# Spacing the loads of a scan by their landings, and reloading 112 of 128 rows

## The chip, the cores and the metric

One core of one Trainium2 chip. The metric is device time of one execution in microseconds, the median over runs; lower is better. The kernel before took 630.66 us (three runs, 629.27 to 634.14).

## The reference

A recurrent attention with a delta rule is followed by a mixture of experts. For 4 batches and 8 heads, 768 steps and head dimension 40, a 40 x 40 state is carried along the steps:

```
y[t]  = r[t] @ state
Sa    = state @ a[t]
state = state * w[t] - outer(Sa, b[t]) + outer(v[t], k[t])
```

The rows y of all batches and steps form x (3072 x 320). Each row picks one of 8 experts by the largest of `x @ w_gate`, takes a place among that expert's rows in order of arrival, goes through `relu(x @ w1[e]) @ w2[e]` (hidden width 1024), and is scaled by its softmax weight.

## The kernel before

**The scan** works on six stages of 128 steps (index `i`, `NI` = 6), each in two halves of 64 steps (`c`) and for two groups of heads and batches (`pr`). Within a half, matrices of 64 x 64 replace the step by step recurrence. For each (`pr`, `i`) the inputs come as w (tile `px`), a (tile `a`), k and b (tile `kb`, one load for each half) and r (tile `rv`), each a load of 512 KB or a little more, 128 rows of 4 KB. For each (`pr`, `i`, `c`) v comes as two loads of 128 KB (tile `vu`). VectorE makes running products of w (two scans, L494 and L503) and multiplies them into a (L508) and kb (L513); TensorE forms the products (`nn` and `kk`, L406); VectorE inverts a triangular matrix in many small steps (L641, L646); then TensorE carries the states (`zz`, `sa`, `mT`, `yy`). At a stage's end x goes to HBM (`store_x`, two stores of 192 KB each).

Of the 128 rows of w, a and kb the arithmetic on VectorE uses rows 0 to 103 (`R` = 104): two blocks of 40 rows at 0 and 64. In a and kb the rows 104 to 127 are zeros from the host, and products on TensorE read all 64 rows of a block, zeros included. In w the rows between the blocks are copies that keep the values finite.

**The experts** follow: weights are loaded, split in two half-precision parts by ScalarE and VectorE, x is gathered and transposed by DMA, and TensorE multiplies (L1594 and L1463). The first loads of weights go out while the scan still runs.

**The order** of all steps is written out by hand in `ORDER` (L29). `Schedule.listed` (L202) replays it, so each engine gets its instructions in that order and runs them in that order; costs in the steps' texts, such as `L0>2.0`, are not used when an order is given. All plain loads and stores are issued by SyncE through `Schedule.dma` (L169, the calls show as L171). A load's issue waits for its tile to be free, and everything behind it on SyncE waits too. The first steps that load, in order: w, kb, a, kb, w, kb, a, kb, w, a, v, w, v, rv, v, the gate's weights, a, rv; then, from 33.8 us, kb, kb, kb, w, kb, four stores of zeros (`fill`, xd<-tbl), v, w. The number of buffers is 6 for `px`, 4 for `a`, 2 for `kb`, 2 for `rv` and 4 for `vu` (L365).

The lines that the change touches are `Schedule.__init__` and `dma`, `steps` (L173), the loads in `prep` (L460 to L486) and the step of `store_x` (L1041).

Of the kernel before, what the change touches and what calls it, by code (L numbers as in the profile page):

```python
# [19 lines left out]
P = 128  # L20
C = 64
DIGITS = str.maketrans("", "", "0123456789")


OVERLAP = 0.07
AFTER = {"P": 0.3, "A": 0.05, "V": 0.12, "G": 0.06, "W": 0.06}

# [103 lines left out]
class Schedule:  # L131
# [7 lines left out]
    def __init__(self, nc, bufs, mu, tail, bias, alt=(100.0,) * 3, later={}, given=None):  # L139
        self.nc, self.bufs, self.mu, self.o_tail, self.bias, self.alt = nc, bufs, mu, tail, bias, alt  # L140
        self.later, self.given = later, given
        self.begin = {"A": 12.0, "V": 2.0, "G": 8.0}
        self.threads, self.plan, self.queue, self.pick = {}, [0.0], [], {}

    def get(self, name):
        return self.bufs[name].pop(self.pick[name].pop(0) if self.pick.get(name) else 0)
# [20 lines left out]
            self.nc.vector.tensor_mul(out, in_, m)  # L167

    def dma(self, out, in_):  # L169

        (self.nc.scalar if self.queue.pop(0) == "A" else self.nc.sync).dma_start(out, in_)  # L171

    def steps(self, name):  # L173
        def add(fn, text, needs=(), gives=None, take=(), free=()):
            ops = [[[(y[0], [float(z) - OVERLAP * (y[0] == "V") for z in y[1:].split(">")]) for y in x.split("&")]
                    for x in z.split()] for z in text.split("|")]
            self.threads.setdefault(name, []).append((fn, ops, needs, gives, tuple(take), tuple(free), self.plan[0]))
        return add

# [167 lines left out]
def scan_part(tc, keep, one, psum, w, a, kb, rv, vt, w_gate, wge, xd, lg, ident, up, SX, route, fill):  # L347
    nc = tc.nc
    V, A, G, TT = nc.vector, nc.scalar, nc.gpsimd, nc.tensor
    NI = w.shape[1]  # L350
# [39 lines left out]
             "w": -20.1216, "w_": 0.8755, "x": -104.8416, "x_": -62.5388, "zz": 0.4931}  # L390
    sch = Schedule(nc, free_, MU, O_TAIL, O_BIAS, (1.42109, 1.49794, -0.061783), LATER, ORDER)
    get, put, steps, PLAN, queue = sch.get, sch.put, sch.steps, sch.plan, sch.queue
    engine, copy, scale, dma = sch.engine, sch.copy, sch.scale, sch.dma

    def half(x, n=C):
        return slice(C * x, C * x + n)
# [51 lines left out]
    def masked(out, in_):  # L448
# [7 lines left out]
        else:  # L456
            m = mask[:, None, :] if len(sh) == 3 else mask[:, None, None, :]
            V.tensor_mul(out, in_, m.to_broadcast(sh))  # L458

    def prep(pr, i):  # L460
        T = {"pr": pr, "i": i}
        n = (pr, i)

        def loads(kind, src, rows):
            def go():
                T[kind] = get(kind)
                dma(rows(T[kind]), src[pr, i])
            return go

        def load_kb(c):  # L470
            if not c:
                T["kb"] = get("kb")
            dma(T["kb"][:, c].rearrange("p h z t -> p (h z t)"), kb[pr, i, c])

        def load_w():
            T["px"] = get("px")
            dma(T["px"].rearrange("p h t -> p (h t)"), w[pr, i])

        steps("load_w")(load_w, "L0>2.0", take=["px"], gives=("load_w", n))
        steps("load_a")(loads("a", a, lambda x: x.rearrange("p h t -> p (h t)")), "L0>1.9", take=["a"],  # L480
                        gives=("load_a", n))
        for c in range(2):
            steps("load_kb")(lambda c=c: load_kb(c), "L0>1.9", take=["kb"] * (1 - c), gives=("load_kb", n, c))
        PLAN[0] += HC / 2
        steps("load_rv")(loads("rv", rv, lambda x: x.rearrange("p z u t -> p (z u t)")), "L0>1.9",
                         take=["rv"], gives=("load_rv", n))  # L486
        PLAN[0] -= HC / 2

        def scan_g():
            T["gx"] = get("gx")  # L490
            if i:
                T["g0"] = get("g0")
            V.memset(z2[0:R, :, 0:1], 1.0)
            V.tensor_tensor_scan(T["gx"][0:R, 0:H * (P + 1)][:, ::-1],  # L494
                                 T["px"][0:R].rearrange("p h t -> p (h t)")[:, ::-1],
                                 z2[0:R].rearrange("p h t -> p (h t)")[:, ::-1], 1.0, ALU.mult, ALU.add)

        def scan_p():
            g3 = T["gx"][0:R, 0:H * (P + 1)].rearrange("p (h t) -> p h t", t=P + 1)
            if i:  # L500
                V.tensor_copy(T["g0"][0:R, :], g3[:, :, 1])
            V.reciprocal(z2[0:R, :, 0], g3[:, :, 1])
            V.tensor_tensor_scan(T["px"][0:R].rearrange("p h t -> p (h t)"),  # L503
                                 T["px"][0:R].rearrange("p h t -> p (h t)"),
                                 z2[0:R].rearrange("p h t -> p (h t)"), 1.0, ALU.mult, ALU.add)

        def mul_a():
            engine().tensor_mul(T["a"][0:R], T["a"][0:R], T["px"][0:R, :, 0:P])  # L508

        def mul_kb(c):  # L510
            g = T["gx"][0:R, 1:].rearrange("p (h t) -> p h t", t=P + 1)[:, :, 1:]
            x = T["kb"][0:R, c]
            engine().tensor_mul(x, x, g[:, :, None, half(c)].to_broadcast([R, H, 2, C]))  # L513
            if c:
                put("gx", T["gx"])

        add = steps(f"decay{pr}")
        add(scan_g, "V2.4", take=["gx"] + ["g0"] * (i > 0), needs=[("load_w", n)], gives=("gx", n))
        add(scan_p, "V2.6", gives=("px", n))
        add(mul_a, "V1.22|G2.35", needs=[("load_a", n)], gives=("a", n))  # L520
        add = steps(f"decay_k{pr}")
        for c in range(2):
            add(lambda c=c: mul_kb(c), "V1.15|G2.35", needs=[("px" if c else "gx", n), ("load_kb", n, c)], free=["gx"] * c, gives=("kb", n, c))
        return T
# [454 lines left out]
    def gate(T):  # L979
        pr, i = T["pr"], T["i"]  # L980
        n = (pr, i)
        Q = {}

        def turn_y():
            p = Q["pt"] = get("pp")
            for h in range(H):
                TT.transpose(p[:, h // 4, h % 4 * P:h % 4 * P + R], T["px"][0:R, h, 0:P], ident[0:R, 0:R])  # L987

        def logits():
            p = Q["pl"] = get("p1")  # L990
            for h in range(H):
                mm(p[32 * (h % 4):32 * (h % 4) + 16, 0:P], wge[:, h].rearrange("p x e -> p (x e)"), T["px"][:, h, 0:P], h < 4)

        def parts():
            copy(T["px"][:, 0, 0:P], Q["pl"][:, 0:P])

        def fold():
            mm(Q["pl"][:, P:P + 16], T["px"][:, 0, 0:P], pick, True)
            put("px", T["px"])

        def hv(x):
            return Q["pt"].rearrange("p z (k y) -> p (z k) y", y=P)[:, :, C * x:C * x + D]

        def x_hi():
            Q["x16"] = get("x16")
            for x in range(2):
                copy(Q["x16"][:, x, 0, 0:HD].rearrange("p (h d) -> p h d", d=D), hv(x))

        def x_lo():
            for x in range(2):  # L1010
                V.tensor_sub(Q["x16"][:, x, 1, 0:HD].rearrange("p (h d) -> p h d", d=D), hv(x),
                             Q["x16"][:, x, 0, 0:HD].rearrange("p (h d) -> p h d", d=D))
            put("pp", Q["pt"])

        def x_rest():
            y = Q["x16"]
            copy(y[:, :, 1, HD:], y[:, :, 0, 2 * P:HD])
            copy(y[:, :, 0, HD:], y[:, :, 1, 2 * P:HD])

        def take_logits():  # L1020
            scale(lg[:, i * B + pr:i * B + B:2, :], Q["pl"][:, P:P + 16].rearrange("p (x e) -> p x e", x=2), 1.0 / SX)
            put("p1", Q["pl"])

        def store_x():
            for x in range(2):
                t = (pr + 2 * x) * NI + i
                dma(xd[i == NI - 1][t * P:(t + 1) * P, :], Q["x16"][:, x].rearrange("p a c -> p (a c)"))
            put("x16", Q["x16"])

        add = steps(f"gat{late(i)}{pr}")  # L1030
        done = [("y", (pr, 2 * i)), ("y", (pr, 2 * i + 1))]
        add(turn_y, "P1.0", needs=done, take=["pp"], gives=("turn_y", n))
        more = steps(f"logi{late(i)}{pr}")
        more(logits, "P.5", needs=done + [("wge", 0)], take=["p1"])
        more(parts, "A.25|V.25", needs=[("turn_y", n)])
        more(fold, "P.25", free=["px"])
        more(take_logits, "A.2|V.2", free=["p1"], gives=("logits", n))
        add(x_hi, "A.46 A.46|V.49 V.49", take=["x16"])
        add(x_lo, "V.49 V.49", free=["pp"])
        add(x_rest, "A.3 A.3|G.76 G.76")  # L1040
        add(store_x, "L0>.55&L0>.55", needs=[("fill", 0)] * (i == NI - 1), free=["x16"], gives=("store_x", n))  # L1041

    Ts = {}
    for i in range(NI):
# [26 lines left out]
    for m, G_ in enumerate(sets):  # L1071
        PLAN[0] = G_[-1] * GT + 1.5 * GT
        add = steps(f"rout{late(G_[-1])}")
        L_ = {}
        first, count, place, gates, hot_p, hot_j, fold, index = route(m, G_, L_)
        n = len(G_)
        add(first, f"V{1.1 + .2 * n:.2f}", needs=[("logits", (pr, i)) for pr in range(2) for i in G_] + [("gated", m - 1)] * (m > 0),
            gives=("one_hot", m))
        add(lambda f=count, L=L_: (L.update(ps=get("p1")), f()), "P.5", take=["p1"], gives=("counted", m))
        add(lambda f=place, L=L_: (f(), put("p1", L["ps"])), f"V{.6 + .15 * n:.2f}", needs=[("placed", m - 1)] * (m > 0),  # L1080
            free=["p1"], gives=("placed", m))
# [705 lines left out]
```

## Time and profile before

| | before |
|---|---|
| median of three runs | 630.66 us |
| the profiled execution | 628.57 us |
| its span, first to last instruction | 626.8 us |
| TensorE busy (matmul) | 536.7 us, 86% |
| TensorE instructions, matmuls and weight loads | 12512 and 12512 |
| VectorE instructions | 855 |
| VectorE busy | 415.9 us, 66% |
| ScalarE busy | 279.1 us, 45% |
| mean granted TensorE clock | 0.941 |
| DMA, SyncE's queue | 71.91 MB, 39.4% of 16 engines |
| HBM read | 66.39 MB |

The profiled execution took 1.8 us more than its span. Busy shares are means over a scan in which VectorE and TensorE are both above eight tenths busy, and a last third in which TensorE alone is. PE is TensorE's matmuls, PEld its weight loads, DVE is VectorE, ACT ScalarE, POOL GpSimd, SP SyncE; a q behind the name means the engine's sequencer.

### The profile page before, as it was taken

What the parts mean: (1) busy time and instruction counts of PE and PEld (TensorE: products, weight loads), DVE (VectorE), ACT (ScalarE), POOL (GpSimd) and SP (SyncE); (2) the same over time, 40 slices, a digit from 0 to 9 for tenths busy, and PEclk for the clock granted to TensorE, in tenths of its full rate; (3) what the DMA queues carried; (4) which work ended last, traced back from release to release, by engine and by line L of the source; (5) the groups of instructions that cost most, each with busy time, mean ns of one, the idle gap of its engine ahead of it and who ended that gap; (6) DMA issues with size and microseconds to landing.
All of it is one profiled execution on the core that took longest, in us unless ns stands there. A gap on an engine that the chain in (4) does not pass through costs nothing.

```text
span 626.8 us, 27526 instructions
## 1 busy us (share of the span) xinstructions
PE 536.7 (86%) x12512; PEld 394.2 (63%) x12512; DVE 415.9 (66%) x855; ACT 279.1 (45%) x559; POOL 113.4 (18%) x148
## 2 busy tenths in 40 slices
PE   2476988878899898899899898889999969879995
PEld 1365876667677666777688667656766445535653
DVE  7899987887578877488788857956436555142420
ACT  5246534724364455335745345544247334244221
POOL 7110000101010001001010000414152733506102
PEclk9855998999799998799999988989999999989999
DMA  8672152413442524235122426594588868484001
GB/s 345 179 202 72 35 160 91 140 62 101 158 130 87 158 77 138 76 117 157 60 80 73 142 75 198 132 238 125 98 253 227 237 165 210 109 209 117 21 18 37
DMA packets 67219, 83.22 MB, mean 133 GB/s; under 512 B 30590, under 2 KB 54272, under 8 KB 67092
## 3 DMA queue, kind: packets, MB, share of 16 engines
q1 hardware_dynamic: 63764, 71.91, 39.4%
q0 software_dynamic: 3328, 9.44, 5.2%
q8 instruction: 100, 1.64, 1.1%
q14 instruction: 27, 0.22, 0.1%
HBM read 66.39 MB, written 10.09 MB: 122 GB/s over the span
## 4 chain that ended last, share of the span: by engine, by line
PE 54%; issue 23%; DVE 11%; POOL 5%; DMA 3%; ACT 2%; POOLq 0%; SPq 0%; DVEq 0%; ACTq 0%
PE pp L406 27%; PE pp L1594 6%; PE pp L199 5%; PE p L1463 4%; PE pp L851 3%; POOL out_dram L1469 3%; PE p L199 2%; PE pp L562 2%; PE p L406 2%; PE pp L987 1%; POOL a L1440 1%; PE p L889 1%; DVE gx L494 1%; DVE nu L646 1%; DVE tmp L641 1%
## 5 line engine op out<-in xcount | busy, mean ns | idle before, releaser
L406 PE MATMUL pp<-a,kb 64*64 64x64 f32 x1536 | 36.8, 243 | 21.5 <-DVE a L508 7.9
L1469 POOL DMA_INDIRECT out_dram<-tk,ri x25 | 32.2, 1287 | 119.6 <-ACT tk L1629 95.0
L406 PEld LDWEIGHTS pp<-a,kb 64*64 64x64 f32 x1536 | 31.6, 154 | 29.2 <-issue 11.1
L199 PE MATMUL pp<-ident 128*128 128x512 f16 x126 | 43.0, 416 | 4.1 <-ACT pp L424 3.2
L156 POOL COPY x<-x 128x128 f16<-128x128 f16 x12 | 6.5, 540 | 210.6 <-ACT x L156 191.0
L1440 POOL DMA_INDIRECT a<-xd,ri x25 | 29.3, 1171 | 83.7 <-PE pp L987 73.8
L406 PE MATMUL pp<-vu,bk 128*40 128x104 f32 (+1 forms) x768 | 39.7, 257 | 2.4 <-issue 2.1
L406 PEld LDWEIGHTS pp<-vu,bk 128*40 128x40 f32 x768 | 34.2, 120 | 6.6 <-issue 4.5
L458 DVE TENSOR_TENSOR vu<-pp,mask 128x1024 f32<-128x1024 f32 x24 | 29.3, 1221 | 9.8 <-PE pp L406 9.7
L156 ACT COPY vT<-pp 128x1024 f32<-128x1024 f32 x22 | 22.2, 1014 | 30.4 <-PE pp L851 30.3
L570 ACT ACTIVATE bk<-pp,few 128x320 f32<-128x320 f32 x48 | 22.6, 524 | 29.0 <-PE pp L562 19.8
L406 PE MATMUL pp<-rv,vT 64*64 64x64 f32 x1536 | 29.7, 221 | 5.2 <-issue 3.6
L160 ACT ACTIVATE ns<-pp 32x256 f32<-32x256 f32 (+1 forms) x54 | 24.3, 450 | 21.6 <-PE pp L406 20.7
L1594 PE MATMUL pp<-xT,kb 128*128 128x448 f16 (+2 forms) x192 | 32.2, 306 | 0.0
L1594 PE MATMUL pp<-xT,px 128*128 128x448 f16 (+2 forms) x128 | 28.6, 315 | 3.9 <-DMA xT<-a 3.9
L406 PEld LDWEIGHTS pp<-rv,vT 64*64 64x64 f32 x1536 | 25.6, 134 | 8.1 <-issue 3.8
L851 PE MATMUL pp<-ident,vu 128*128 128x128 f32 x192 | 28.2, 294 | 2.2 <-issue 2.1
L1594 PE MATMUL pp<-xT,vu 128*128 128x448 f16 (+1 forms) x128 | 26.2, 370 | 3.8 <-DVE px L1602 3.8
L494 DVE TENSOR_TENSOR_SCAN gx<-px,z 104x1032 f32<-104x1032 f32 x12 | 27.7, 2308 | 2.4 <-DMA px<-in_w_dram 1.9
L513 DVE TENSOR_TENSOR kb<-kb,gx 104x1024 f32<-104x1024 f32 x22 | 27.1, 1252 | 3.1 <-DMA kb<-in_kb_dram 3.1
L641 DVE TENSOR_TENSOR tmp<-xu,nu 128x60 f32<-128x60 f32 (+11 forms) x138 | 28.0, 227 | 1.5
L646 DVE TENSOR_TENSOR nu<-nu,tmp 128x60 f32<-128x60 f32 (+11 forms) x138 | 27.7, 225 | 1.7
(262 smaller groups left out, 1361.5 us busy)
## 6 DMA issues: line engine op xcount, KB each, us to landing
kb<-in_kb_dram SPq DMA_DIRECT2D x24, 512.0 KB, 4.9
vu<-in_moe_w_dram SPq DMA_DIRECT2D x32, 320.0 KB, 3.6
px<-in_w_dram SPq DMA_DIRECT2D x12, 516.0 KB, 5.9
a<-in_a_dram SPq DMA_DIRECT2D x12, 512.0 KB, 4.0
vu<-in_vt_dram SPq DMA_DIRECT2D x48, 128.0 KB, 3.4
rv<-in_rv_dram SPq DMA_DIRECT2D x12, 512.0 KB, 4.7
px<-in_moe_w_dram SPq DMA_DIRECT2D x12, 512.0 KB, 4.7
xd<-x SPq DMA_DIRECT2D x24, 192.0 KB, 2.9
```

What stands on the lines that cost most here:

```text
L156: (e.copy if e is self.nc.scalar else e.tensor_copy)(out, in_)
L199: self.nc.tensor.matmul(x, self.spare[:, 0:P], self.spare[:, None, :].to_broadcast([P, 2, 2 * P]), start=True, stop=True, skip_group_check ...
L406: TT.matmul(out, l, r, start=start, stop=True, skip_group_check=True)
L458: V.tensor_mul(out, in_, m.to_broadcast(sh))
L494: V.tensor_tensor_scan(T["gx"][0:R, 0:H * (P + 1)][:, ::-1], T["px"][0:R].rearrange("p h t -> p (h t)")[:, ::-1], z2[0:R].rearrange("p h t ...
L513: engine().tensor_mul(x, x, g[:, :, None, half(c)].to_broadcast([R, H, 2, C]))
L641: V.tensor_mul(tv(), diag(s_["xu"])[:, :, t0:t1, s:s + 1].to_broadcast([P, nb, n, m]), diag(s_["nu"])[:, :, s:s + 1, 0:m].to_broadcast([P, ...
L646: V.tensor_add(y, y, tv())
L851: TT.transpose(p[:, x, k * P:k * P + P], U["vu"][:, x, k, C:3 * C], ident)
L1440: nc.gpsimd.indirect_dma_start(out=xt(j)[:c].rearrange("p a c -> p (a c)"), out_offset=None, in_=src[:, :], in_offset=bass.IndirectOffsetO ...
L1469: nc.gpsimd.indirect_dma_start(out=out_v[used[0] % (8 * E)][:, :], out_offset=bass.IndirectOffsetOnAxis(ap=ri.bitcast(U32)[:c, j, 1:2], ax ...
L1594: nc.tensor.matmul(s_["h", f + z][:, :n], l, rr, start=m % 7 == 0 and m < 14, stop=m >= 14)
```

## The change

Two things are changed. First, each step of the scan that loads (`load_w`, `load_a`, `load_kb`, `load_rv`, `load_v`, and the load of the gate's weights), and each `store_x`, waits on SyncE until the last DMA of the second last such step has landed. Steps of loads for the experts and the four stores of `fill` neither wait so nor count. Second, a tile of w, a or kb that has been loaded once with all 128 rows is from then on reloaded in its rows 0 to 111. That holds for 6 of 12 loads of w, 8 of 12 of a and 20 of 24 of kb. The order of the steps is the same.

```diff
+LANDED = mybir.DependencyInfo(mybir.DependencyClass.Sync, mybir.DependencyReason.DATA)
...
+        self.spaced, self.loads = False, [[] for _ in range(3)]
...
     def dma(self, out, in_):
-
-        (self.nc.scalar if self.queue.pop(0) == "A" else self.nc.sync).dma_start(out, in_)
+        x = (self.nc.scalar if self.queue.pop(0) == "A" else self.nc.sync).dma_start(out, in_)
+        if self.spaced:
+            for y in self.loads[0][-1:]:
+                self.tc.add_manual_dep(x.ins, y.name, LANDED, reason="loads are spaced")
+            self.loads[-1].append(x.ins)
+
+    def load(self, fn):
+        self.spaced, self.loads = True, self.loads[1:] + [[]]
+        fn()
+        self.spaced = False
 
     def steps(self, name):
...
+            if name.startswith("load_"):
+                fn = lambda fn=fn: self.load(fn)
...
+    whole = set()
+
     def prep(pr, i):
...
+        def part(kind, x, src):
+            y = slice(0, 112 if kind != "rv" and id(T[kind]) in whole else P)
+            dma(x[y], src[y])
+
         def loads(kind, src, rows):
             def go():
                 T[kind] = get(kind)
-                dma(rows(T[kind]), src[pr, i])
+                part(kind, rows(T[kind]), src[pr, i])
+                whole.add(id(T[kind]))
             return go
 
         def load_kb(c):
             if not c:
                 T["kb"] = get("kb")
-            dma(T["kb"][:, c].rearrange("p h z t -> p (h z t)"), kb[pr, i, c])
+            part("kb", T["kb"][:, c].rearrange("p h z t -> p (h z t)"), kb[pr, i, c])
+            if c:
+                whole.add(id(T["kb"]))
 
         def load_w():
             T["px"] = get("px")
-            dma(T["px"].rearrange("p h t -> p (h t)"), w[pr, i])
+            part("px", T["px"].rearrange("p h t -> p (h t)"), w[pr, i])
+            whole.add(id(T["px"]))
...
-        add(store_x, "L0>.55&L0>.55", needs=[("fill", 0)] * (i == NI - 1), free=["x16"], gives=("store_x", n))
+        add(lambda: sch.load(store_x), "L0>.55&L0>.55", needs=[("fill", 0)] * (i == NI - 1), free=["x16"], gives=("store_x", n))
```

## Rows read from the trace of the kernel before

**Rows 1.** Page, part 4: shares of the chain that ended last, by engine.

```profile
PE 54%; issue 23%; DVE 11%; POOL 5%; DMA 3%; ACT 2%; POOLq 0%; SPq 0%; DVEq 0%; ACTq 0%
```

**Rows 2.** Waits of PE, whole run: us in total, times, longest us.

```profile
PE pp L406 <- issue: 29.6, 33, 2.6
```

**Rows 3.** Chain in order of time, pieces without cause: start us, us.

```profile
97.09 1.58 issue
...
161.32 2.37 issue
...
183.78 1.18 issue
...
250.29 2.56 issue
```

**Rows 4.** DMA by queue (packets, MB, share), whole run, then 25 to 400 us.

```profile
q8 instruction: 100, 1.64, 1.1%
...
q8 instruction: 85, 1.39, 1.5%
```

**Rows 5.** DMA by queue, 156.9 to 161.3 us, then 161.3 to 162.4 us.

```profile
q1 hardware_dynamic: 400, 1.46, 88.8%
...
q8 instruction: 1, 0.02, 5.8%
```

**Rows 6.** Timeline of SP, issues: start us, us, what, count.

```profile
39.70 6.71 SPq L171 DMA_DIRECT2D xd<-tbl  x4
...
89.84 3.04 SPq L171 DMA_DIRECT2D kb<-in_kb_dram  x3
...
155.04 0.33 SPq L171 DMA_DIRECT2D rv<-in_rv_dram  x1
155.42 0.83 SPq L171 DMA_DIRECT2D kb<-in_kb_dram  x1
156.33 0.38 SPq L171 DMA_DIRECT2D px<-in_w_dram  x1
156.77 2.57 SPq L171 DMA_DIRECT2D kb<-in_kb_dram  x2
...
177.44 2.07 SPq L171 DMA_DIRECT2D vu<-in_vt_dram  x2
...
246.96 0.88 SPq L171 DMA_DIRECT2D rv<-in_rv_dram  x1
```

**Rows 7.** DMA issues at 155.5, 156.4 and 156.8: KB, us from issue to landing.

```profile
kb<-in_kb_dram SPq DMA_DIRECT2D x1, 512.0 KB, 5.8
...
px<-in_w_dram SPq DMA_DIRECT2D x1, 516.0 KB, 6.2
...
kb<-in_kb_dram SPq DMA_DIRECT2D x1, 512.0 KB, 7.4
```

**Rows 8.** DMA by queue, 186.5 to 191.7 us, all of it; then PE's timeline.

```profile
q8 instruction: 1, 0.02, 1.1%
...
192.80 0.38 PE L406 MATMUL pp<-vu,bk 128*40 128x104 f32 x4 [0.83 <-issue]
```

**Rows 9.** DMA issues at 1.0 and at 33.9 us, as in rows 7.

```profile
px<-in_w_dram SPq DMA_DIRECT2D x1, 516.0 KB, 3.5
...
kb<-in_kb_dram SPq DMA_DIRECT2D x1, 512.0 KB, 3.8
```

**Rows 10.** Timeline of DVE at the start.

```profile
13.19 2.31 DVE L494 TENSOR_TENSOR_SCAN gx<-px,z 104x1032 f32<-104x1032 f32 x1
...
21.53 2.31 DVE L494 TENSOR_TENSOR_SCAN gx<-px,z 104x1032 f32<-104x1032 f32 x1
25.48 1.92 DVE L755 STREAM_TRANSPOSE xu<-ns 128x1024 f32<-128x1024 f32 x1 [1.64 <-ACT ns L160]
```

**Rows 11.** Waits of DVE, 0 to 400 us, for a load, past the first.

```profile
DVE kb L513 <- DMA kb<-in_kb_dram: 3.1, 1, 3.1
```

**Rows 12.** Waits of SP's own queue, whole run.

```profile
SPq L171 <- PE pp L406: 122.6, 24, 25.8
```

More of the change, by code (lines that the diff above doesn't have):

```diff
@@ L392, in scan_part @@
     get, put, steps, PLAN, queue = sch.get, sch.put, sch.steps, sch.plan, sch.queue
+    sch.tc = tc
     engine, copy, scale, dma = sch.engine, sch.copy, sch.scale, sch.dma
@@ L472, in load_kb @@
                 T["kb"] = get("kb")
-            dma(T["kb"][:, c].rearrange("p h z t -> p (h z t)"), kb[pr, i, c])
+            part("kb", T["kb"][:, c].rearrange("p h z t -> p (h z t)"), kb[pr, i, c])
+            if c:
+                whole.add(id(T["kb"]))
         def load_w():
             T["px"] = get("px")
-            dma(T["px"].rearrange("p h t -> p (h t)"), w[pr, i])
-        steps("load_w")(load_w, "L0>2.0", take=["px"], gives=("load_w", n))
-        steps("load_a")(loads("a", a, lambda x: x.rearrange("p h t -> p (h t)")), "L0>1.9", take=["a"],
+            part("px", T["px"].rearrange("p h t -> p (h t)"), w[pr, i])
+            whole.add(id(T["px"]))
+        steps("load_w")(load_w, "L0>1.75", take=["px"], gives=("load_w", n))
+        steps("load_a")(loads("a", a, lambda x: x.rearrange("p h t -> p (h t)")), "L0>1.68", take=["a"],
                         gives=("load_a", n))
         for c in range(2):
-            steps("load_kb")(lambda c=c: load_kb(c), "L0>1.9", take=["kb"] * (1 - c), gives=("load_kb", n, c))
+            steps("load_kb")(lambda c=c: load_kb(c), "L0>1.68", take=["kb"] * (1 - c), gives=("load_kb", n, c))
         PLAN[0] += HC / 2
```

## The prediction

> **What bounds the kernel now.** I read the chain that ended last first: by engine it is TensorE for half, and "issue" for almost a quarter [rows 1], that is time in which an engine waited for nothing that the profile names. The waits of PE tell whose: its matmuls stood 33 times for such a reason, 29.6 us in all [rows 2]. The chain in order of time shows that the long ones in the scan lie on the path [rows 3]. Next I asked what DMA does beside them. Queue 8 moves nothing but instructions, 100 packets of 16 KB, 85 of them between 25 and 400 us, one each 375 / 85 = 4.4 us [rows 4]. Only TensorE has instructions in that number, 25,000 of them. The gap at 161.32 then reads so: from 156.9 to 161.3 us only SyncE's queue moves, 400 packets, and not one of queue 8; the code packet comes just when the gap begins, and PE goes on 1.3 us after that packet's window ends [rows 3, 5]. So TensorE ran out of code, and the code came behind loads. The reader is to see five loads issued between 155.04 and 159.3 [rows 6].
>
> Loads as data are hardly waited for: behind the very first, VectorE waits for one in the whole scan, a kb, for 3.1 us [rows 11]. It is that of 155.42, in the same stretch as PE's gap, and the path there goes over PE [rows 3]. So the change is worth what it does to the code.
>
> **The change part by part.**
>
> (1) Loads kept apart. Before, loads leave as soon as their tiles are free; after, at most two steps are under way. What one transfer holds up is read from the burst: issue plus time to landing gives 155.42 + 5.8 = 161.2, 156.33 + 6.2 = 162.5 and 156.77 + 7.4 = 164.2, so each load of 512 KB takes 1.3 to 1.7 us behind the one before [rows 6, 7]. Three of the long gaps fall where more than two load steps were under way: 97.09 (three kb in a row from 89.84), 161.32, and 183.78 (two v from 177.44 between a w and an rv) [rows 3, 6]. They sum to 1.58 + 2.37 + 1.18 = 5.13 us. The new wait takes one transfer out from before the fetch in the first and third, two at 161.32: at most 1.3 + 2.37 + 1.18 = 4.85 us. The least is nothing: if the fetch was asked for before the later loads were issued, nothing is taken from before it. A fetch with no load beside it still costs something: between 186.5 and 191.7 us queue 8 alone has a packet, and PE stands 0.83 us after it [rows 8]. I take the gaps down to that: 0.75 + 1.54 + 0.35 = 2.6 us, the row nearest to a fetch that finds a short queue. All of it is on the path [rows 3]. The gap of 2.56 us at 250.29 has one rv ahead, from 246.96, and a store of x before it, which the new wait lets pass [rows 3, 6]; it stays, and so do most of the 33.
>
> (2) 112 rows. One eighth less of a load is 1.3 / 8 = 0.16 us. The 34 loads that shrink are a quarter of the 134 DMAs of the steps concerned. If each of the 33 gaps [rows 2] had one of them ahead, the gain would be 5.3 us; if none, zero. A quarter of 33 gives 8 x 0.16 = 1.3 us, which I take. VectorE's, ScalarE's and TensorE's work on the rows is the same and costs the same.
>
> (3) The start. The first nine loads are w, kb, a, kb, w, kb, a, kb, w; each now leaves as the one two before it lands. With t for a load's time to landing, the second w lands at 4.3 + 2t and the third at 4.3 + 4t. VectorE begins on them at 13.19 and 21.53 [rows 10], so nothing is late while t stays under 4.45 and 4.3 us. Loads with few beside them took 3.5 and 3.8 [rows 9]; at 3.8 the two land at 11.9 and 19.5. I take zero. If that cover went, with t = 5.8 as in the burst [rows 7], the second w would be 2.7 late; the third would be 6.0 late, of which 2.7 are in already and 1.64 are VectorE's own idle time before 25.48 [rows 10]: 2.7 + 1.7 = 4.4 us in all.
>
> (4) The second burst, from 33.8 us: kb, w and kb wait for one another, and the four stores of zeros behind them, which SyncE took 6.71 us to issue from 39.70 on, start later [rows 6]. By two loads of 1.3, that is 2.6 us. Nothing reads the zeros soon, and the v and w queued behind them are the next stage's. But a fetch of code then meets these stores where it met none. Between 0 and 2.6 I take 1.0 us against the change, the size of a fetch's lone gap of 0.83 [rows 8] rounded up.
>
> (5) Everything else at nothing. SyncE already stands 122.6 us for TensorE to free tiles [rows 12]; outside the bursts the second last load has landed by then, and the new wait is over before the old one. Behind a waiting load on SyncE stand later loads, stores of x and, late in the scan, loads of weights for the experts, whose tiles come free one by one as well. What VectorE, ScalarE and TensorE are given does not change, and neither does its order.
>
> Sum: -2.6 - 1.3 + 0 + 1.0 = -2.9 us. The profiled execution of 628.57 would become 625.7. It lies 2.1 us under the median of the runs; against the median, 630.66 - 2.9 = 627.8 us.
>
> [...]
>
> **The rivals.**
>
> More than forecast: the depth of the queue is what holds the code up everywhere. Then (1) and (2) give their upper ends, 4.85 + 5.3, and (4) nothing: 630.66 - 10.2 = 620.5 us. For it: PE's gaps are on the path, and 33 of them. Against it: the gaps at 192.80 and 250.29 had no or hardly any load too many [rows 3, 8].
>
> [...]
>
> Slower: apart, loads are slower. Two at a time and 3.8 us for each pair is 1.9 us a load against 1.3 [rows 7, 9]. A burst of five loads then lasts 9.5 us and not 6.5. It decides when a burst outlasts two distances of fetches, 8.8 us [rows 4]: a third fetch then meets traffic, in each of the five stages after the first. At the size of the smallest of the chain's gaps, 1.18 us [rows 3], that is 5.9 us, with no gain elsewhere: 636.6 us. Against it: a fetch has at most two loads ahead, and PE runs some us on the code it has.
>
> **How the numbers follow.** Forecast 0.45, more 0.25, no change 0.18, slower 0.12. The time is the forecast's, 627.8. The range goes from 621, close to the second case, over the third to 634, where the start's 4.4 us or part of the slower case are in; it leaves out some 0.18. About 1%, 6.3 us, is what runs of this kernel can tell from no change. Faster by more than that, under 624.4, is most of the second case and a little of the first: 0.25. Slower, over 637, is half of the last case and a little for a shift of the order that nobody sees in the trace: 0.10. Within: 0.65.
>
> **What would show it.** (1) is right if the gaps without cause near 97, 161 and 184 shrink to under a microsecond and the sum of rows 2 falls by 3 to 5 us; wrong if the code packets come as late as before. (2): kb, w and a of 448 KB land some tenths earlier. (3) is wrong if VectorE's scans near 13 and 21 us wait for a load. (4) shows as a new gap of PE between 45 and 55 us. The prediction falls if the sum of rows 2 halves, or if it grows with more and smaller gaps.

## The result and the profile after

| | before | after |
|---|---|---|
| median, first comparison (20 runs each) | 629.73 us | 629.37 us |
| median, second comparison (29 and 12 runs, the run e1 below) | 631.89 us | 625.39 us |
| the profiled execution | 628.57 us | 630.85 us |
| waits of PE without cause, all tiles | 32.6 us | 32.7 us |
| PE busy, matmul | 536.7 us | 533.1 us |
| HBM read | 66.39 MB | 64.16 MB |

The ratio after to before is 0.9891, 95% interval 0.9849 to 0.9932, in the first comparison and 0.9898, 0.9847 to 0.9948, in the second. In the first it is further from 1 than the ratio of the medians, because it counts only the runs of each kernel within 1.5% of its fastest, 18 of 20 before and 8 of 20 after. By medians the change gained 0.4 us in the first comparison and 6.5 us in the second. So these runs show a gain between nothing and 1%, at the edge of what can be told from none. The forecast was 627.8 us, between the two medians.

The profiled execution after lies 1.5 us above its median, so it is read for where code and loads meet, and not for its length. First the waits of PE (us in total, times, longest us), which answer to [rows 2]; PE's L419 is L406 of before, and L874 is L851:

```profile
PE pp L419 <- issue: 28.4, 36, 2.0
PE pp L874 <- issue: 4.1, 5, 1.3
PE p L419 <- issue: 0.2, 1, 0.2
```

The longest gap is shorter, and there are more of them; the sum has not moved (before, the three lines were 29.6, 2.1 and 0.9). Next the shares of the chain, for [rows 1], and its pieces without cause over 1 us between 140 and 260 us, for [rows 3]:

```profile
PE 53%; issue 23%; DVE 12%; POOL 5%; DMA 4%; ACT 2%; POOLq 0%; SPq 0%; DVEq 0%; ACTq 0%
```

```profile
144.59 1.38 issue
173.90 1.16 issue
197.63 1.13 issue
202.41 1.72 issue
220.60 1.83 issue
235.18 1.85 issue
244.95 1.32 issue
249.72 2.02 issue
```

The pieces of before at 97.09 and 161.32 are gone and the one at 183.78 is still 1.16 at 173.90. The piece at 220.60 is new, that at 235.18 was 1.17 at 238.03, and that at 244.95 was 0.46 us between starts before. The burst that caused the gap at 161 now looks like this, SyncE's issues first, for [rows 6], then the DMA queues from 153.3 to 157.0 us, for [rows 5]:

```profile
151.52 0.35 SPq L172 DMA_DIRECT2D rv<-in_rv_dram  x1
151.95 0.57 SPq L172 DMA_DIRECT2D kb<-in_kb_dram  x1
155.76 0.31 SPq L172 DMA_DIRECT2D px<-in_w_dram  x1
156.83 3.19 SPq L172 DMA_DIRECT2D kb<-in_kb_dram  x2
```

```profile
q1 hardware_dynamic: 248, 0.89, 71.0%
q8 instruction: 1, 0.02, 2.0%
```

w leaves 3.8 us after kb where it left 0.9 us after it, and the code packet is in after 248 packets of loads, where 400 had gone by and none of code had come. VectorE's scans at the start, for [rows 10], its wait for kb in that burst, for [rows 11], and the waits of SP's own queue, for [rows 12]:

```profile
13.31 2.31 DVE L517 TENSOR_TENSOR_SCAN gx<-px,z 104x1032 f32<-104x1032 f32 x1
...
21.64 2.31 DVE L517 TENSOR_TENSOR_SCAN gx<-px,z 104x1032 f32<-104x1032 f32 x1
```

```profile
156.84 1.23 DVE L536 TENSOR_TENSOR kb<-kb,gx 104x1024 f32<-104x1024 f32 x1 [2.01 <-DMA kb<-in_kb_dram]
```

```profile
SPq L172 <- PE pp L419: 102.9, 23, 19.3
...
SPq L172 <- DMA vu<-in_vt_dram: 22.6, 15, 3.1
SPq L172 <- DMA kb<-in_kb_dram: 22.0, 15, 2.6
```

The scans start 0.1 us later than before and wait for nothing. The new wait is real: SyncE stands 22.0 us for landings of kb, where it stood 2.6 us, and 22.6 for those of v, where it stood 0.3; it stands for TensorE 20 us less.

### The profile page after: what moved, and what is told of

The parts are those of the page before. It is cut to its first block, busy times and chain, and to the rows that moved or that the text cites. A ratio compares the mean times of both kernels' runs of the same rounds, so it can differ in the third digit from the quotient of the medians.

```text
span 629.1 us, 27527 instructions
## 1 busy us (share of the span) xinstructions
PE 533.1 (85%) x12512; PEld 389.8 (62%) x12512; DVE 416.2 (66%) x855; ACT 279.2 (44%) x559; POOL 113.3 (18%) x148
## 3 DMA queue, kind: packets, MB, share of 16 engines
q8 instruction: 100, 1.64, 1.1%
HBM read 64.16 MB, written 10.09 MB: 118 GB/s over the span
## 4 chain that ended last, share of the span: by engine, by line
PE 53%; issue 23%; DVE 12%; POOL 5%; DMA 4%; ACT 2%; POOLq 0%; SPq 0%; DVEq 0%; ACTq 0%
PE pp L419 27%; PE pp L1617 6%; PE pp L211 4%; PE p L1486 4%; PE pp L874 3%; POOL out_dram L1492 3%; PE p L211 2%; PE pp L585 2%; POOL a L1463 1%; PE pp L1010 1%; PE p L419 1%; DMA vu<-in_moe_w_dram 1%; PE p L912 1%; DVE gx L517 1%; DVE nu L669 1%
## 5 line engine op out<-in xcount | busy, mean ns | idle before, releaser
L419 PE MATMUL pp<-a,kb 64*64 64x64 f32 x1536 | 38.1, 247 | 20.7 <-DVE kb L536 8.0
L419 PEld LDWEIGHTS pp<-a,kb 64*64 64x64 f32 x1536 | 32.5, 158 | 28.9 <-issue 10.0
L419 PE MATMUL pp<-vu,bk 128*40 128x104 f32 (+1 forms) x768 | 39.9, 257 | 1.3 <-issue 1.3
L419 PEld LDWEIGHTS pp<-vu,bk 128*40 128x40 f32 x768 | 34.2, 120 | 5.1 <-issue 3.3
L471 DVE TENSOR_TENSOR vu<-pp,mask 128x1024 f32<-128x1024 f32 x24 | 29.3, 1219 | 10.5 <-PE pp L419 10.5
L419 PE MATMUL pp<-rv,vT 64*64 64x64 f32 x1536 | 30.3, 225 | 6.8 <-issue 4.3
L162 ACT ACTIVATE ns<-pp 32x256 f32<-32x256 f32 (+1 forms) x54 | 24.3, 450 | 23.6 <-PE pp L419 22.7
L419 PEld LDWEIGHTS pp<-rv,vT 64*64 64x64 f32 x1536 | 26.3, 138 | 9.3 <-issue 4.2
L874 PE MATMUL pp<-ident,vu 128*128 128x128 f32 x192 | 26.4, 279 | 4.1 <-issue 4.1
L526 DVE TENSOR_TENSOR_SCAN px<-px,z 104x1032 f32<-104x1032 f32 x12 | 27.7, 2307 | 0.4
```

What stands on the lines that cost most here:

```text
L419: TT.matmul(out, l, r, start=start, stop=True, skip_group_check=True)
L874: TT.transpose(p[:, x, k * P:k * P + P], U["vu"][:, x, k, C:3 * C], ident)
```

## The experiments

Theory: TensorE's code comes behind whatever loads are under way, so the depth of the queue of loads sets how long TensorE stands without code. Rivals: spacing does nothing to the code; or the smaller loads are the whole effect. A third rival is not in the edits at all: TensorE's granted clock differs from run to run (0.918 to 0.957 in the runs of before beside e1 to e4), and with it the time. Two readings are used throughout, both set out here for all runs. One is the gap before PE's instruction 7,873, which is the gap at 161 us of before. The count begins at 0 and takes all of TensorE's records in order of start: matmuls, weight loads and 74 others, such as semaphore instructions. The gap is given as the time between the starts of that instruction and of the one before it. The other is how much a kernel wins or loses against the profile of before between PE's instructions 7,000 and 16,000, 147.4 and 299.9 us there. Beside it stand what of that is less busy time of PE and what is less waiting without cause, and the mean granted clock of the stretch, where 1 is full speed; the one lower level in the records of before and after is 0.5.

| run | steps under way | median us | before, beside it | gap at 7,873 | won from 7,000 to 16,000 | of it PE busy | of it without cause | clock there | PE without cause, all |
|---|---|---|---|---|---|---|---|---|---|
| before | no limit | | | 2.56 | | | | 0.94 | 32.6 |
| e3 rows only | no limit | 630.02 | 631.89 | 3.88 | 0.8 | 2.0 | -1.2 | 0.95 | 32.6 |
| e5 | 3 | 630.01 | 630.14 | 3.41 | -0.2 | 0.2 | -0.8 | 0.94 | 31.3 |
| after | 2 | 629.37 | 629.73 | 0.25 | -2.6 | 1.1 | -3.0 | 0.96 | 32.7 |
| e1 again | 2 | 625.39 | 631.89 | 1.58 | 2.5 | 0.9 | 1.8 | 0.95 | 28.6 |
| e2 spacing only | 2 | 625.13 | 631.89 | 0.49 | 4.8 | 5.5 | 0.2 | 0.99 | 31.3 |
| e6 104 rows | 2 | 625.95 | 630.14 | 1.62 | 0.9 | 1.0 | -0.5 | 0.94 | 29.2 |
| e4 | 1 | 662.60 | 631.89 | 0.04 | 11.9 | 6.3 | 9.6 | 0.99 | 18.8 |
| e7 | 2, then 1 | 626.32 | 630.14 | 0.40 | 7.8 | 4.1 | 7.3 | 0.96 | 23.7 |
| e8 | 2, then 1, kb 2 | 618.78 | 630.14 | 0.41 | 11.0 | 6.7 | 4.6 | 0.99 | 23.6 |
| e9 as e8 | 2, then 1, kb 2 | 622.18 | 631.52 | 0.42 | 9.9 | 5.5 | 4.5 | 0.98 | 27.4 |
| e10 | as e8 from step 18 | 620.55 | 631.52 | 0.38 | 13.4 | 7.4 | 6.8 | 1.00 | 23.5 |
| e11 as e8, 128 rows | 2, then 1, kb 2 | 621.64 | 631.52 | 0.38 | 10.4 | 7.4 | 3.4 | 1.00 | 30.0 |
| e12 as e8, stores free | 2, then 1, kb 2 | 620.80 | 631.52 | 0.49 | 8.3 | 6.4 | 2.5 | 0.99 | 30.3 |

The clock is why "won" can't be read as code alone. This is the stretch in before and in e2 (us, then busy us of PE, PEld, DVE, ACT and POOL with the number of instructions, the clock, DMA's share and GB/s):

```profile
147.40:299.90 152.50, 135.09 (x4504) 109.93 (x4501) 114.31 (x228) 73.74 (x161) 10.95 (x10) 0.94 0.38 119
147.70:295.40 147.70, 129.59 (x4505) 105.56 (x4503) 113.64 (x228) 73.79 (x161) 11.11 (x10) 0.99 0.40 120
```

All that e2 won there is less busy time of the same matmuls at 0.99 of the clock and not 0.94; its waits without cause are those of before. Over whole runs the clock matters as much. One straight line with a common slope through the runs of before, e1, e2 and e3 has a run take 3.6 us less for each 0.01 more of its mean. An estimate from these runs puts all kernels of a comparison at an equal mean clock, by such a line, without one run of 974 us (e9) and one of 774 us (e10), for which no run gives a cause. Against before they then stand at -1.6 us (e3) and +0.3 (e5) with no limit or three; -4.1 (e1), -5.2 (e2) and -3.8 (e6) with two; -3.7 (e7), -7.1 (e8), -6.1 (e9), -9.8 (e10), -6.2 (e11) and -7.1 (e12) with one after the start; each give or take 2 to 3 us. So the clock alone doesn't make the gains. How much of them is code is another question: PE's waits without cause fall by 1.3 to 4.0 us in e1, e2 and e6 and not at all in the first profile.

**e1, the change again.** No edit.

> The changed kernel once more, unaltered, as the measure for the three beside it. Theory (the code of TensorE comes behind loads; the change takes some of its long waits away and puts new, middling ones in their place): within 1% of the kernel before, ratio 0.99 to 1.00; waits of PE without cause 28 to 34 us in all, as before (29.6). Rival (the loads' spacing is a plain gain): ratio under 0.99 and these waits under 26 us.

Ratio 0.9898 (0.9847 to 0.9948). Its profiled execution took 622.06 us, 8.8 us less than that of the first, with the same code and the same mean granted clock of 0.952. Its waits of PE:

```profile
PE pp L419 <- issue: 25.2, 40, 1.5
PE pp L874 <- issue: 2.5, 2, 1.4
PE p L419 <- issue: 0.9, 1, 0.9
```

These sum to 28.6 us, 4.1 less than in the first profile: about half of the 8.8. The gap that had looked new there, at 220.60, is 2.02 us between starts in the first profile and 0.10 here, as before; that at 235.18 is 1.36 before, 2.04 in the first profile and 1.67 here. Between instructions 7,000 and 16,000 the first profile lost 2.6 us and this one won 2.5. So one trace of this kernel places a stretch of 150 us to no better than some 5 us, and the loss in the first trace can't be put down to the change.

**e2, the spacing alone.**

```diff
-            y = slice(0, 112 if kind != "rv" and id(T[kind]) in whole else P)
+            y = slice(0, P)
```

> The spacing alone, every load with all 128 rows. Theory: PE's gap near 161 us (2.37 before) goes under 1.2, the code packet there comes earlier, and gaps of over 1 us turn up where a burst now lasts longer (195 to 255 us); waits of PE without cause 28 to 36 us; ratio to before 0.995 to 1.005. [...] Rival B (all of the change is in the smaller loads): ratio 1.00 here and the whole gain in the run of rows alone.

Ratio 0.9891 (0.9848 to 0.9935), so the spacing alone gains as much as the whole change; the theory's own range of 0.995 to 1.005 missed it and rival B is refuted; that spacing does nothing to the code is refuted by the gap at 7,873, 0.49 us for 2.56. Gaps also stand where the theory put new ones: before instructions 12,737 and 12,993, at 243 and 247 us, PE stands 1.79 and 1.54 us, for 0.01 and 0.46 before. But e3, which has no spacing, has 0.97 and 1.26 there, so it isn't shown that the spacing made them. The gap at 7,873 is in PE's timeline (start us, us, operation, count, and in brackets the idle time before it):

```profile
161.82 0.22 PE L419 MATMUL pp<-xu,yq 64*48 64x16 f32 x2 [0.30 <-issue]
```

**e3, 112 rows alone.**

```diff
             for y in self.loads[0][-1:]:
-                self.tc.add_manual_dep(x.ins, y.name, LANDED, reason="loads are spaced")
+                pass
```

> 112 rows alone, no spacing. Theory: the burst at 155 to 164 us is there as before, one eighth shorter, so the gap near 161 stays between 1.5 and 2.4 us; the sum of PE's waits without cause falls by 0.5 to 2 us from 29.6; ratio 0.996 to 1.000. Rival B (the smaller loads carry the change): ratio and waits as in the changed kernel. Rival C (a load's bytes don't matter): nothing moves by more than 0.3 us.

Ratio 0.9956 (0.9913 to 0.9999), by medians 1.9 us, at equal clock 1.6 give or take 2: hardly told apart from nothing. The waits of PE sum to 32.6 us as before, and the gap at 7,873 has grown, beyond the range expected. First its row, then the queues from PE's instruction 7,579, which starts at 160.0, to the end of the code packet at 166.2 us:

```profile
167.54 0.27 PE L419 MATMUL pp<-xu,yq 64*48 64x16 f32 x2 [3.69 <-issue]
```

```profile
q1 hardware_dynamic: 498, 1.82, 97.8%
q8 instruction: 1, 0.02, 1.3%
```

498 packets of loads went by before the code packet was in, and PE stood 3.69 us. At this place smaller loads without spacing do not let the code through.

**e4, one step at a time.**

```diff
-        self.spaced, self.loads = False, [[] for _ in range(3)]
+        self.spaced, self.loads = False, [[] for _ in range(2)]
```

> 112 rows, and each load waits for the landing of the last one, so that one at a time is under way. Theory: a fetch of code has one load ahead at most, so no wait for code over 1.5 us comes from a burst of the scan, but bursts last half as long again (3.8 us a load against 1.9), loads come late at the start and at 157 us, and VectorE waits for loads, 5 to 20 us in all: slower than the changed kernel by 1 to 3%. Rival (code is free of the loads' depth): waits for code as in the changed kernel, and the same late loads.

5.4% slower (4.9 to 5.9). The waits of PE and of DVE, whole run:

```profile
PE pp L419 <- issue: 17.2, 25, 1.5
PE pp L874 <- issue: 1.4, 2, 0.8
```

```profile
DVE kb L536 <- DMA kb<-in_kb_dram: 46.3, 12, 15.3
DVE gx L517 <- DMA px<-in_w_dram: 7.7, 4, 2.4
DVE a L531 <- DMA a<-in_a_dram: 3.3, 2, 2.2
```

Both halves of the theory show in this kernel. TensorE stands for code 18.8 us and not 32.6, never over 1.5; VectorE stands 57 us for loads, three times the upper end expected. By instruction 7,000 it is 36.2 us behind before, and by 16,000 it has won 11.9 of these back. The rival, that code does not care how many loads are ahead, is not borne out. Yet this run alone doesn't refute it, since its TensorE was also late, by those 36.2 us, and what that does to the waits for code is not shown; e8, which is not late, is the cleaner test.

**e5, three under way.**

```diff
-        self.spaced, self.loads = False, [[] for _ in range(3)]
+        self.spaced, self.loads = False, [[] for _ in range(4)]
```

> Each load waits for the landing of the third last, so up to three are under way. Theory (what lies ahead of a code packet sets its wait): between the kernel before and the change; PE's waits without cause 28 to 33 us, the gap near 161 us between 1.0 and 2.4; ratio to before 0.992 to 1.000. Rival (a wait of any depth does the same, or the depth doesn't matter): as the change on the same chip, 0.99, or as the kernel before, 1.00, with the gap at 161 unchanged.

Ratio 1.0018 (0.9972 to 1.0064): no gain, just outside the range on that side. The gap and the queues, from instruction 7,579 at 156.0 to 161.7 us:

```profile
163.06 0.22 PE L419 MATMUL pp<-xu,yq 64*48 64x16 f32 x2 [3.22 <-issue]
```

```profile
q1 hardware_dynamic: 443, 1.62, 98.5%
q8 instruction: 1, 0.02, 1.4%
```

With three under way the burst of five is hardly held back: 443 packets ahead of the code. Between three and two, this gap drops from over 3 us to 0.25 to 1.62 in four profiles. "In between" was wrong: here it is a step.

**e6, 104 rows.**

```diff
-            y = slice(0, 112 if kind != "rv" and id(T[kind]) in whole else P)
+            y = slice(0, 104 if kind != "rv" and id(T[kind]) in whole else P)
```

> The change with 104 rows reloaded and not 112. [...]

Median 625.95 against 630.14, ratio 0.9974 (0.9936 to 1.0012). The packets of one lone load of kb, here and in e1:

```profile
DMA packets 117, 0.43 MB, mean 112 GB/s; under 512 B 13, under 2 KB 13, under 8 KB 117
```

```profile
q1 hardware_dynamic: 128, 0.46, 36.9%
```

117 is 104 rows and 13 packets under 512 B; 128 is 112 rows and 16 such packets. Which engines they went on, and where a code packet waits, no view shows. The gap at 7,873 is 1.62 us, for 1.58 in e1. The trace gives no landing times for these loads.

**e7, two at the start, then one.** From the 45th load step on, about 148 us, a load waits for the last one.

```diff
-            for y in self.loads[0][-1:]:
+            for y in self.loads[int(self.count > 44)][-1:]:
```

> The change, but from the 45th load step on (about 148 us) one load at a time is under way, as in the run with one at a time all through; the start is as in the change. Theory: that run lost 35 us by 125 us and won back about 13 us against the kernel before between 147 and 306 us, where the change won 4 in its second profile; so this one should be 2 to 8 us faster than the change, 617 to 624 us, with PE's waits without cause at 18 to 23 us. Rival: what that run won back was only slack that its late start had left, and here the late loads of kb (VectorE waited 1 to 5 us for each in that run) cost as much as the code gives: 625 to 632 us.

626.32 us against 630.14, ratio 0.9953 (0.9906 to 1.0000), between theory and rival. Waits of PE, then of DVE from 150 to 400 us:

```profile
PE pp L421 <- issue: 21.0, 32, 1.7
```

```profile
DVE kb L538 <- DMA kb<-in_kb_dram: 17.2, 5, 5.6
DVE gx L519 <- DMA px<-in_w_dram: 1.0, 1, 1.0
```

The code's part comes as said: 23.7 us without cause in all, and 7.3 us less of it between instructions 7,000 and 16,000. The late loads of kb take it back, in five waits of up to 5.6 us. The last two of them, 2.6 and 5.6 us at 298 and 306 us, stand where the lead over before falls, from 10.7 us at instruction 16,000 to 2.6 at 22,000.

**e8, and kb two at a time.** As e7, with the loads of kb waiting for the second last step again.

```diff
-            for y in self.loads[int(self.count > 44)][-1:]:
+            for y in self.loads[int(self.count > 44 and not self.kb)][-1:]:
```

> As the run before, but loads of kb wait for the second last step as in the change; all other steps from the 45th on wait for the last. Theory: the loads that VectorE waits for come 2 to 4 us earlier, and code packets meet two loads at a time only behind a kb: 615 to 623 us, VectorE's waits for kb under 8 us in all after 150 us. Rival: pairs with kb are where the long waits for code are, and their sum stays at 25 us or more: as the change, 624 to 628 us.

618.78 us against 630.14; ratio 0.9890 (0.9837 to 0.9942). Its waits:

```profile
PE pp L422 <- issue: 19.7, 29, 1.5
PE pp L877 <- issue: 3.5, 3, 1.8
```

```profile
DVE kb L539 <- DMA kb<-in_kb_dram: 1.9, 1, 1.9
```

TensorE's waits for code stay down, 23.6 us, and VectorE's 17.2 us for kb are 1.9. The lead is 12.6 us at instruction 16,000 and 10.5 at the end; between 7,000 and 16,000 it wins 4.6 us by shorter waits without cause and 6.7 by PE's busy time at the higher clock. It has the lowest median of all, though by its ratio it is not told apart from the change.

**e9 to e12, on one chip.** e9 is e8 unaltered; the others each alter it in one thing.

```diff
# e10
-            for y in self.loads[int(self.count > 44 and not self.kb)][-1:]:
+            for y in self.loads[int(self.count > 17 and not self.kb)][-1:]:
# e11
-            y = slice(0, 112 if kind != "rv" and id(T[kind]) in whole else P)
+            y = slice(0, P if kind != "rv" and id(T[kind]) in whole else P)
# e12
-        add(lambda: sch.load(store_x), "L0>.55&L0>.55", ...
+        add(store_x, "L0>.55&L0>.55", ...
```

> The best version so far (one load step under way from the 45th on, loads of kb two) once more, unaltered. Theory: 617 to 623 us, PE's waits without cause 22 to 26 us, as in its first profile (23.6); 8 to 12 us under the kernel before in the median. Rival (its first profile was a lucky one): 624 to 629 us.

> As the best version, but one at a time (loads of kb two) from the 18th step on, about 55 us, and not from the 45th. Theory (each pair of loads costs code somewhere): 0 to 4 us faster than the best version, PE's waits without cause 20 to 24 us, by the fetches between 55 and 147 us. Rival (the second stage's loads have no slack): VectorE waits for w, a or kb between 60 and 130 us, over 5 us in all, and the time is 2 to 10 us over the best version.

> As the best version, but every load with all 128 rows. Theory (the 112 rows are worth a term of 1.3 us by the forecast, and 1.1 us measured alone): 0 to 2 us slower than the best version. Rival (with loads one at a time, each load's length counts fully, 0.2 us on 34 loads): 3 to 7 us slower.

> As the best version, but the stores of x neither wait nor count: a store leaves as soon as it may, and the load behind it too. Theory: stores add to what lies ahead of a code packet, 24 of 192 KB in all; PE's waits without cause rise by 1 to 3 us, and the loads behind the stores come 2 us earlier, which nobody needs: 0 to 3 us slower. Rival (a store doesn't hold code up, since its packets go the other way): the same or up to 3 us faster, without VectorE's wait of 1.9 us for a store of x.

e9: 622.18 us, ratio 0.9893 (0.9848 to 0.9938), and 27.4 us without cause, a little over its range. It is 9.3 us under before by medians; e8 had been 11.4 under. e10: 620.55 us, ratio 0.9832 (0.9760 to 0.9904), six runs; its 23.5 us without cause are as its theory had them. Its DVE waits between 55 and 150 us, and the one on the chain:

```profile
DVE kb L539 <- DMA kb<-in_kb_dram: 4.9, 2, 3.5
```

```profile
97.42 4.07 DMA kb<-in_kb_dram
```

It is 5.9 us behind before at instruction 7,000, where e9 is 2.3 ahead, and 7.5 ahead at 16,000. At the end it is 8.5 ahead, e9 8.7. What the second stage loses the later ones win: 6.8 us of it are shorter waits without cause, and 7.4 are PE's busy time, at a granted clock of 1.00. e11: 621.64 us, ratio 0.9889 (0.9819 to 0.9958), level with e9: the 112 rows are worth nothing that shows. e12: 620.80 us, ratio 0.9874 (0.9805 to 0.9943), level with e9 too; 30.3 us without cause is 2.9 more than in e9, as expected, but e11 has 30.0 with no such edit, and VectorE's wait for a store of x is gone, as its rival said. One place speaks for a store's part: before instruction 13,249, where two stores of x are issued just ahead of an rv, e12 has 432 packets of its queue pass and a gap of 2.51 us, where e8, e9 and e11 have 288 to 333 packets and 1.05 to 1.41 us. In the sum it is not settled. All four agree with one another within their intervals, though e11 and e12 stand for code about as long as e2 and e5 do, whose medians are 4 to 9 us longer: their profiles are ahead of that of before by less busy time of PE, 531.0 and 526.7 us for 536.7, at a mean clock of 0.953 and 0.964 for 0.941, more than by code.

## Why the prediction held, and where it did not

The time was right: 627.8 us forecast, medians of 629.37 and 625.39 measured, inside the range and within 1% or at its edge. Some of that is luck. Steps (1), (2) and (4) were each off, on different sides: the spacing is worth more than its 2.6 us by time, and the 1.3 us of the rows and the 1.0 us against the change do not show. And the same change gained 0.4 us in one comparison and 6.5 us in the other, so neither alone could tell 2.9 us from nothing.

Step (1) held at one of its three places. It took 2.6 us from the three gaps; between the starts of the instructions they were 1.77, 2.56 and 1.39 us before, and 0.48, 0.25 and 1.12 in the profile after, 3.9 us less; in e1 2.8 and in e2 3.1 less. The sign named, all three under a microsecond, came in none of them. The one at 161 follows the depth in every kernel of the table: 2.56 to 3.88 us with three steps or no limit, 0.25 to 1.62 with two, at most 0.49 with one (in e8 to e12 kb two). The other two do not. That at 97 is 0.13 us in e5 with three under way, and 1.28 and 1.59 in e9 and e11 with two. That at 184 is 0.01 us in e3, without any limit, and 1.67 in e2. The other sign, a sum of [rows 2] lower by 3 to 5 us, was seen once (25.2 in e1) and once not (28.4): one trace was too few for it. By time, the spacing is worth more than its three gaps: e2's median is 6.8 us under that of before, 5.2 at equal clock, where the step said 2.6. The code waits that went, 1.3 us in e2's profile, do not account for that.

Step (2) was over-counted. It gave 1.3 us; the rows alone measured 1.9 us by medians, within the noise, and on top of the spacing nothing (625.39 with, 625.13 without; 622.18 and 621.64 with one under way). Its sign, smaller loads of kb landing earlier, is the spacing's: kb takes 4.6 us after and 4.9 before, but 4.6 in e2 with all 128 rows and 5.1 in e3 with 112 and no spacing. What the gap at 161 us follows is how many loads are under way, by the figures above; what an eighth off each is worth is too little to see.

Step (3) held: the scans at 13.31 and 21.64 wait for nothing. Where its cover goes, e4 shows: w, a and kb then come late one after another, and the kernel is 36.2 us behind at instruction 7,000.

Step (4) failed. It forecast a new gap between 45 and 55 us, 1.0 us. The stores of zeros start even later than was said, at 46.67 and not 39.70:

```profile
46.67 4.04 SPq L172 DMA_DIRECT2D xd<-tbl  x4
```

But at the three places between 45 and 55 us where TensorE needs a code packet it stands 0.01, 0.14 and 0.01 us. Nothing was lost to them.

Step (5) held for VectorE: its wait for kb is 2.01 us, for 3.05 before. It was wrong that the new wait is over before the old one outside the bursts: SyncE stands 22.6 us for landings of v and 22.0 for kb. VectorE's waits for kb do not grow by it: 2.2 us in all, for 3.1 before. The other cases: "no change", given 0.18, is not borne out, by the gap at 161 and by the times of e2 and e8. "More than forecast" has a cause that shows in part, but two under way isn't enough for it; with one under way after the start and kb at two the medians come to 618.8 to 622.2, the neighbourhood of the 620.5 us that it gave. Its sum was all code, and of that e8's profile shows 9.0 us, e11's and e12's 2.6 and 2.3. "Slower", by stretched bursts, is what happened to kb in e7 and to everything in e4, not in the change.

What stays open is why two executions of the same code place their gaps so differently (28.6 and 32.7 us), and which part of the second comparison's 6.5 us is not waits for code. The clock is part of it: at equal clock 4.1 us are left of e1's gain. PE's busy time fell from 536.7 to 533.1 and 532.4 us in the two profiles of the change, at a mean granted clock of 0.952 for 0.941; whether the spacing raises the clock, by sparing TensorE long gaps, or only met it higher, no run here isolates.

## What to carry to other kernels

When the chain shows an engine standing without cause, look at the instruction queue beside it: if code packets come when a burst of loads ends, limit the burst's depth first, and its bytes after that. Limit how many loads are under way where they have slack, and let those pass whose data is needed next; at the start, where everything is needed, one at a time cost 36 us. Before a gap in one trace is called an effect of the change, look for it in a second trace of the same kernel. And before a stretch is called won, compare TensorE's granted clock and busy time in it: here up to 7 us of 150 came from there.

## What the runs showed of the hardware

TensorE's gaps without cause stand at fixed places in its program, before the instructions 449 + 256 n, counted as above, the same in every kernel, and end 0.9 to 1.8 us after the end of packet n of queue 8 (n from 0; 423 gaps over 0.5 us before 400 us, in fourteen profiles). That TensorE runs out of code there is read from this match. A packet is 16 KB (1.64 MB in 100 packets, [rows 4]); over 256 instructions that is 64 bytes each, an estimate from these two numbers. The earliest start of a code packet in any profile is 294 instructions before the one that needs it; 7,579 is that point for 7,873 (n = 29). When TensorE asks for a packet no profile shows. From there to the end of the code packet the numbers of load packets that passed, and the gaps, are: 517 and 2.56 us (before), 498 and 3.88 (e3), 443 and 3.41 (e5), 274 and 0.49 (e2), 260 and 1.58 (e1), 248 and 0.25 (after), 111 and 0.40 (e7). The last is here, from 155.1 to 158.0 us, with the row of PE:

```profile
q1 hardware_dynamic: 111, 0.39, 34.1%
q8 instruction: 1, 0.02, 2.1%
```

```profile
159.09 0.22 PE L421 MATMUL pp<-xu,yq 64*48 64x16 f32 x2 [0.21 <-issue]
```

Counted so for all 1,111 code packets between 25 and 400 us in the fourteen profiles: where fewer than 100 packets of SyncE's queue passed, none of 381 gaps is over 1.5 us and 9 are over 1; where 100 or more passed, 87 of 730 are over 1.5 and 196 over 1. So in these profiles no gap over 1.5 us came with less traffic than that, and traffic alone did not make one: of the 257 with 400 or more, 177 have a gap under 1 us.

In before the granted clock falls to half right after the gaps at 97 and 161 us. These two stretches have 0.51 and 0.52; that from 102.6 to 163.8 us, between them, has 1.00:

```profile
99.00:102.50 3.50, 3.50 (x101) 3.46 (x94) 1.50 (x2) 0.00 (x0) 0.00 (x0) 0.51 0.02 5
164.00:171.00 7.00, 7.00 (x130) 5.83 (x125) 5.31 (x7) 2.13 (x6) 0.00 (x0) 0.52 0.04 13
```

Between 66 and 340 us of the fourteen profiles, such a fall begins within 4 us of 12 of the 15 code gaps of over 2 us, and of 6 of the 566 under 0.5 us. Falls without such a gap exist too (e7 at 162.3 us). What sets the clock no run isolates.

PE's waits without cause sum to 18.8 to 32.7 us a run in these profiles. A load of 112 rows is 128 packets of the profile (e1, above), so the 443 and 498 that passed in e5 and e3 are over three loads. How many of them were ahead of the code packet's request is not shown.
